# Last rows in 32-row transfers on two queues, two thirds of the angles together, and a new order of all steps

## The chip, the cores and the metric

The kernel runs on one core of a Trainium2 chip. A core has TensorE (PE in the profile), VectorE (DVE), ScalarE (ACT), GpSimd (POOL) and SyncE (SP), each with its own instruction stream, and 16 DMA engines that they share. The metric is the device time of one execution in microseconds (us), given as the median of three runs.

## The reference

Eight batches of 576 positions go through linear attention with 8 heads of 64, a norm over each head, and then a gated long convolution; all inputs and the output are float32.

```python
kv  = einsum('bhsd,bhse->bhde', k, v)          # 64x64 per head
out = einsum('bhsd,bhde->bhse', q, kv)
x   = out / sqrt(mean(out*out) + 1e-6) * g_norm  # then (batch, 576, 512)
x1, x2, x3 = split(x @ w_proj, 3)              # 512 columns each
conv = irfft(rfft(x2, 576) * rfft(filter, 576), 576)
y   = (x1 * conv * x3) @ w_out                 # (8, 576, 512)
```

## The kernel before

The work of a batch is cut into some ninety small steps, each a Python function that records a few instructions. The string `ORDER` names the steps one after another, as name.batch, with a third number where filler matmuls stand ahead of the step's own. The loop at the end of the kernel (line 798) calls them in that order, so `ORDER` alone sets the order of the instructions on every engine; the waits between engines follow from the tiles that they share. An engine runs its own instructions strictly in order. PSUM is held as four pairs of banks, and `take` (line 98) gives a step the pair that has been free longest; `free` gives it back when its contents have been copied out.

The steps that the prediction speaks of:

- **Loads.** `L...` steps issue the loads of q, k, v and the weights from GpSimd. `Zi` makes index rows there, `Zd` an identity matrix (`ident`), `Zr` turns it into `rev` on VectorE.
- **Tables.** `An0`, `An1`, `An2` call `angles` (line 227): per third of the frequencies three VectorE instructions and three ScalarE ones (Sin, Abs, Sin) fill `IV`, the table of sines and cosines. `Act` (line 244) loads ScalarE's second function table, which the norm's reciprocal square root needs. `Tb0` to `Tb2` transpose `IV` on TensorE and copy the result out, `Ff0` to `Ff2` fold the filter into `ff` (lines 309 to 324), `H0` to `H2` make the filter's spectrum from both.
- **A batch.** `K` forms kv, `O01` and `O23` the attention, `sq`, `R`, `rs`, `x` the norm, `Ga` and `Gb` the two gates x1 and x3 (line 640, a quarter of the channels each), `abM`, `rrM`, `F0`, `F1`, `F2` the forward transform of x2, `M0` to `M2` its product with the filter, `A0`, `A1` sums on GpSimd or, as `Av0`, `Av1`, on VectorE (line 621), `I` and `Io` the inverse transform, `f...` the last product into `yg`.
- **Output.** `U0`, `U2`, `U4` multiply `yg` by w_out, `ot` copies the result into one of five buffers, and SyncE sends it out in transfers of 32 rows (lines 732 and 745).
- **The last batch's end.** For batch 7 five tiles of 128 rows go another way: `V0` to `V3` (line 759) and `U4` multiply, `va`/`vv` (line 765) copy the tile to SBUF on ScalarE or VectorE, and `V_out` (line 772) sends it in two transfers, one of them of two or three times 32 rows: `[[2 * DM, n], [6 * DM, 32], [1, DM]]`. The step's name has the queue (s SyncE, g GpSimd, a ScalarE), then tile and piece: `dg31` is GpSimd's transfer of piece 1 of tile 3.

Tiles `kb`, `vb` and `sq`, which held k, v and squares before, serve as the output buffers of these five tiles.

Of the kernel before, what the change touches and what calls it, by code (L numbers as in the profile page):

```python
# [19 lines left out]
ORDER = """Z.0 Lqa.0 Zi.0 Lf.0 Zt.0 An2.0 An1.0 An0.0 Zd.0 Act.0 Zf.0 Zr.0 T0.0.18 Tb2.0 Lqb.0 Tb0.0 eTv0.0 Lva.0 Tb1.0.3 Ff0.0  # L20
Ff1.0 Ff2.0.2 Lka.0 Lvb.0 T1.0 Ka.0 Lkb.0 eKva.0 Lw3.0 eTa1.0 H1.0 O01.0 sq1.0 Lqa.1 Kb.0.7 sq0.0 Lw1.0 eKab.0 O23.0
ov0.0 sq3.0 ov1.0 R0.0.1 ov3.0 sq2.0 R1.0.2 rs0.0 ov2.0 R2.0 Lk.1 rs2.0 T0.1 R3.0.1 rs1.0 rs3.0 eTa0.1 Lv.1 x0.0 x1.0
eo1.0 H0.0 H2.0 Gb3.0 Ga3.0 HN1.0 Lqb.1 Ga1.0 eo0.0 K.1 x13.0 Lw2.0 g3.0 eK.1 Gb1.0 fr.0 Ga2.0 x11.0 T1.1 g1.0 HN0.0
x12.0 O01.1 rrM.0 rrT.0 eTa1.1 fa1.0 sq1.1 fa0.0 sq0.1 ob1.1 verr.0 abM.0 F0.0 abT.0 ov0.1 Lv.2 Lkb.2 eab.0 O23.1.2
eT.0 F2c.0 M0.0 F2.0 sq2.1 ob2.1 Lqa.3 Gb2.0 Lqb.3 Lka.2 F1t.0 Lq.2 M2.0 sq3.1 A0.0 F1.0 g2.0 R0.1 ob3.1 R2.1 Ga0.0
rs0.1 R1.1 rs2.1 x10.0 K.2 M1.0 R3.1 Gb0.0 Av1.0 rs1.1 rs3.1 x.1 eo.1 eK.2 I01.0 Io01.0 ea01.0 oa01.0 Io23.0.1 Qt.3
Qt.2 oa23.0 fr.1 I23.0 Qh.3 Ga0.1 ea23.0 g0.0 fa.1 vB.0 Ga1.1 w.0 f001.0 x11.1 rrM.1 x10.1 rrT.1 err.1 O01.2 Lk.3
f101.0 abT.1 sq0.2 ob0.2 f023.0 abM.1 sq1.2 Lvb.4 eT.1 Gb1.1 F0.1 ob1.2 g1.1 eab.1 O23.2 Lv.3 sq2.2 ob2.2 M0.1 Ga3.1
Lwo.0 sq3.2 Gb0.1 F2c.1 f123.0 ob3.2 F2.1 R3.2 x13.1 F1t.1 g0.1 R0.2 F1.1 rs3.2 M2.1 R2.2 rs0.2 rs2.2 R1.2 K.3 Gb3.1
rs1.2 Ga2.1 M1.1 g3.1 eK.3 O23.3 x12.1 sq2.3 sq3.3 Gb2.1 x.2 Lk.4 A0.1 Av1.1 Lva.4 ob3.3 U0.0 Io23.1 g2.1 I23.1 ob2.3  # L30
ot0.0 I01.1 eo0.2 Ga0.2 eo1.2 ea23.1 ea01.1 Lqb.5 fa0.2 ov23.1 Io01.1 R2.3 Lqa.5 oa01.1 fa1.2 xv0.2 abT.2 rs2.3 eT.2
O01.3 fr.2 abM.2 sq0.3 ob0.3 Ga3.2 rrM.2 vB.1 sq1.3 ob1.3 eab.2 R3.3 rrT.2 w.1 x13.2 f001.1 f101.1 f123.1 f023.1 rs3.3
Lqa.4 K.4 F1t.2 err.2 F1.2 eKm.4 R0.3 rs0.3 Gb0.2 M1.2 g0.2 F0.2 Gb3.2 Lqb.4 Ga1.2 U4.1 g3.2 x11.2 R1.3 rs1.3 A1.2
Ga2.2 F2c.2 Lk.5 Lv.5 M0.2 A0.2 Qt.4 Qt.5 ot4.1 x12.2 O23.4 F2.2 x.3 sq2.4 U2.0 ob2.4 Qh.5 M2.2 sq3.4 ot2.0 Gb2.2
I01.2 ov3.4 eo.3 Lqa.6 ea01.2 I23.2 Lqa.7 ea23.2 g2.2 Gb1.2 g1.2 fa0.3 Io23.2 Lqb.6 fa1.3 Io01.2 oa01.2 R3.4 oa23.2
U0.1 rs3.4 Lqb.7 abT.3 fr.3 O01.4 ot0.1 sq1.4 vB01.2 vB23.2 abM.3 sq0.4 veT.3 rrM.3 ob0.4 rrT.3 eab.3 F2c.3 w.2 K.5
ov1.4 err.3 F1t.3 F2.3 F1.3 R2.4 eK.5 rs2.4 fin.2 U2.1 M2.3 M1.3 Ga1.3 F0.3 R1.4 x1.4 ot2.1 x11.3 R0.4 Ga2.3 rs1.4
rs0.4 Gb1.3 x12.3 M0.3 O23.5 g1.3 Lv.6 Gb2.3 sq2.5 Ga3.3 Av0.3 x0.4 ob2.5 g2.3 U0.2 sq3.5 x13.3 Lk.6 A1.3 I23.3 eo0.4
eo1.4 I01.3 ob3.5 ot0.2 Ga0.3 ev23.3 fa0.4 fa1.4 ea01.3 Io01.3 x10.3 Io23.3 ov01.3 fr.4 oa23.3 Gb0.3 g0.3 abT.4 eT.4
K.6 O01.5 vB.3 Gb3.3 eK.6 sq1.5 ob1.5 sq0.5 abM.4 ob0.5 eab.4 w.3 rrM.4 rrT.4 F1t.4 Qt.7 F1.4 g3.3 R3.5 err.4 rs3.5  # L40
R2.5 Ga2.4 rs2.5 Qt.6 x12.4 R0.5 F0.4 fin.3 M1.4 R1.5 rs0.5 A1.4 M0.4 U2.2 rs1.5 Gb2.4 ot2.2 O23.6 F2c.4 x0.5 x1.5
Qh.7 U4.3 g2.4 sq2.6 Av0.4 F2.4 M2.4 eo0.5 Ga3.4 sq3.6 ob3.6 ob2.6 x13.4 Ga0.4 x10.4 ot4.3 U0.3 ot0.3 eo1.5 Io23.4
fr.5 I23.4 Gb3.4 oa23.4 I01.4 Io01.4 ev23.4 oa01.4 fa.5 g3.4 rrM.5 ea01.4 O01.6 sq0.6 rrT.5 vB.4 ob0.6 err.5 Lv.7
Gb0.4 g0.4 Ga1.4 abT.5 xv1.4 sq1.6 Gb1.4 R0.6 eT.5 w023.4 w001.4 ob1.6 rs0.6 Ga1.5 R3.6 g1.4 x11.5 w123.4 F0.5 abM.5
Lk.7 rs3.6 eab.5 w101.4 fin.4 R2.6 rs2.6 M0.5 Gb1.5 K.7 F1t.5 g1.5 F2c.5 eK.7 F1.5 Ga3.5 F2.5 A0.5 x13.5 U2.3 M1.5
M2.5 ot2.3 R1.6 Gb3.5 Ga2.5 g3.5 rs1.6 O23.7 A1.5 x.6 x12.5 U0.4 Gb2.5 sq3.7 ov3.7 sq2.7 ob2.7 ot0.4 R2.7 Io01.5 eo0.6
oa01.5 eo1.6 Ga0.5 g2.5 I23.5 fa.6 fr.6 rs2.7 x10.5 Io23.5 abT.6 ea23.5 I01.5 ov23.5 abM.6 ea01.5 Gb0.5 veT.6 vB.5
eab.6 O01.7 sq0.7 g0.5 sq1.7 F2c.6 ob1.7 F2.6 rrM.6 rrT.6 M2.6 err.6 F1t.6 w.5 F1.6 Ga0.6 ob0.7 R3.7 x10.6 Ga3.6 rs3.7
M1.6 x13.6 fin.5 F0.6 R1.7 rs1.7 R0.7 Gb3.6 rs0.7 Gb0.6 M0.6 g3.6 g0.6 U0.5 Av0.6 Ga1.6 x.7 U4a.5 A1.6 U4b.5 Io01.6
eo.7 ot0.5 x11.6 Ga2.6 oa01.6 ot4.5 fa0.7 x12.6 Io23.6 I01.6 ea01.6 I23.6 oa23.6 U2.5 Gb2.6 vB01.6 fa1.7 ea23.6 fr.7  # L50
g2.6 vB23.6 Gb1.6 g1.6 abM.7 ot2.5 w.6 rrM.7 eab.7 abT.7 fin.6 rrT.7 F2c.7 eT.7 F1t.7 err.7 F2.7 F1.7 U2.4 M1.7 ot2.4
Ga0.7 F0.7 M2.7 Ga1.7 x11.7 A1.7 Gb0.7 x10.7 U0.6 M0.7 Gb1.7 g0.7 Av0.7 I23.7 ot0.6 Io23.7 g1.7 Io01.7 Ga2.7 ov23.7
oa01.7 ev23.7 I01.7 vB23.7 w123.7 Gb3.7 Ga3.7 ea01.7 vB01.7 U2.6 w023.7 w101.7 w001.7 x13.7 g3.7 Gb2.7 x12.7 ot2.6
f101.7 V2a.7 g2.7 f123.7 V3.7 f001.7 V2b.7 va3.7 va2.7 V1a.7 f023.7 ds20.7 V1b.7 dg31.7 U4a.7 vv1.7 V0a.7 ds11.7
ds10.7 U4b.7 dg21.7 V0b.7 vv4.7 va0.7 ds30.7 dg00.7 ds40.7 ds41.7 ds01.7"""
# [3 lines left out]
def kernel(  # L59
# [167 lines left out]
    def angles(c):  # L227

        if 'ang' not in tmp:
            tmp['ang'] = work.tile([P, 2, 3, TH], FP32, name="ang", tag="tpw1")  # L230
# [2 lines left out]
        vec.tensor_scalar(out=a_, in0=tmp['tv'], scalar1=kturn[:, c:c + 1], scalar2=MAGIC, op0=ALU.mult, op1=ALU.add)
# [2 lines left out]
        act.activation(out=IV[:, 2 * c + 1], in_=a_, func=AF.Sin, scale=W0)
# [596 lines left out]
```

## Time and profile before

| | |
|---|---|
| median of 3 runs | 228.15 us (227.96 to 228.92) |
| the profiled execution | 227.85 us, of which the span from first to last instruction is 226.1 us |
| mean granted TensorE clock | 0.967 |
| TensorE busy | 202.1 us (89%) |
| VectorE busy | 183.6 us (81%) |
| ScalarE busy | 146.9 us (65%) |
| GpSimd busy | 59.2 us (26%) |
| read from and written to HBM | 33.69 MB and 9.44 MB |

The profile shows one execution. A group is named by its line of the kernel, engine, operation and tiles; a row of the timeline has start, duration, engine, line, operation and count, and in brackets the idle time ahead of it and what ended that. A row of the windows has a stretch of time, its length, the busy time and number of instructions of each engine, the granted TensorE clock, the mean busy share of the 16 DMA engines and the rate in GB/s. TensorE's matmuls overlap, so that a busy TensorE need not be TensorE at its peak. GpSimd's and SyncE's transfers are listed with the time of issuing them; the time "to landing" runs from the issue until the data is reported as written.

### The profile page before, as it was taken

Reading aid. Unit: us, or ns where it says so; the run is one execution under the profiler, and the core shown is the slowest. Engines: PE = TensorE matmul, PEld = TensorE weight load, DVE = VectorE, ACT = ScalarE, POOL = GpSimd, SP = SyncE. Lnnn points to the kernel's source line nnn. Section 1 sums busy time; section 2 is a strip of 40 time slices with the busy share of each in tenths; the row PEclk is TensorE's granted clock in tenths of the full one; section 3 lists DMA queues with packets and bytes.
Section 4 is the critical chain, followed back from the end, with each engine's and each line's share of the span. In section 5 each row is a group of like instructions: output and inputs, shape, how many; then the busy total and the mean of one; then the engine's idle time right before and its main releaser. Section 6 shows DMA issues by size and latency. Waiting matters only on the chain.

```text
span 226.1 us, 5000 instructions
## 1 busy us (share of the span) xinstructions
PE 202.1 (89%) x2042; PEld 119.9 (53%) x2042; DVE 183.6 (81%) x283; ACT 146.9 (65%) x235; POOL 59.2 (26%) x65
## 2 busy tenths in 40 slices
PE   7898999999999999999999999999999999995000
...
DMA  4999999999999499999458495005001433314410
GB/s 19 191 206 206 207 206 205 207 177 150 207 204 210 117 169 140 256 243 215 129 123 163 61 227 157 0 19 145 27 0 30 122 84 93 97 44 86 105 62 29
DMA packets 37414, 30.16 MB, mean 133 GB/s; under 512 B 16398, under 2 KB 32782, under 8 KB 37390
## 3 DMA queue, kind: packets, MB, share of 16 engines
...
q1 hardware_dynamic: 19694, 12.59, 23.4%
...
HBM read 33.69 MB, written 9.44 MB: 191 GB/s over the span
## 4 chain that ended last, share of the span: by engine, by line
PE 63%; issue 15%; DVE 5%; ACT 4%; POOL 3%; POOLq 0%; DVEq 0%; ACTq 0%
PE ps L640 21%; PE ps L725 7%; PE ps L552 6%; PE ps L670 4%; PE ps L463 3%; PE ps L456 3%; POOL Y L621 3%; PE ps L538 2%; PE ps L558 2%; PE ps L383 2%; DVE tpw L615 2%; PE ps L338 2%; PE ps L545 1%; PE ps L112 1%; PE ps L596 1%
## 5 line engine op out<-in xcount | busy, mean ns | idle before, releaser
L640 PE MATMUL ps<-x,wp 128*128 128x288 bf16 x512 | 70.8, 286 | 0.1
L640 PEld LDWEIGHTS <-wp 128*128 128x128 bf16 x512 | 48.9, 98 | 17.2 <-issue 1.9
L621 POOL TENSOR_TENSOR Y<-tpw 128x1024 bf16<-128x1024 f32 (+1 forms) x10 | 25.9, 2594 | 105.5 <-DVE tpw L615 105.5
L615 DVE TENSOR_TENSOR tpw<-ps,HH 97x2048 f32<-97x2048 f32 (+1 forms) x16 | 36.6, 2289 | 4.2 <-PE ps L596 2.3
L725 PE MATMUL ps<-wo,yg 128*128 128x512 bf16 x112 | 26.5, 379 | 0.0
L646 ACT CAST x<-ps 128x576 bf16<-128x576 f32 x30 | 19.0, 643 | 11.4 <-PE ps L640 9.7
L648 DVE TENSOR_TENSOR g<-ps,x 128x576 bf16<-128x576 f32 x32 | 23.9, 754 | 2.9 <-PE ps L640 1.8
L562 ACT CAST x<-ps 128x1024 bf16<-128x1024 f32 (+1 forms) x21 | 18.8, 895 | 10.3 <-PE ps L552 6.0
L729 ACT COPY ot<-ps 128x1024 f32<-128x1024 f32 x14 | 14.2, 1014 | 12.4 <-PE ps L725 12.3
L477 ACT ACTIVATE rstd<-ps 128x576 bf16<-128x576 f32 x32 | 20.1, 652 | 2.7 <-PE ps L463 2.4
L466 ACT ACTIVATE sq<-ps 128x576 bf16<-128x576 f32 x32 | 20.0, 653 | 2.2 <-PE ps L456 2.0
L674 ACT CAST ar<-ps 128x576 bf16<-128x576 f32 x25 | 15.1, 645 | 7.7 <-PE ps L671 6.8
L473 ACT ACTIVATE o<-ps,g_col 128x576 bf16<-128x576 f32 x24 | 17.7, 749 | 0.0
L725 PEld LDWEIGHTS <-yg 128*128 128x128 bf16 x112 | 10.8, 98 | 11.3 <-issue 0.5
L670 PE MATMUL ps<-IV,Y 128*128 128x192 bf16 x128 | 15.5, 245 | 0.0
L552 PE MATMUL ps<-wp,ab 128*128 128x512 bf16 x64 | 15.1, 380 | 0.0
L140 POOL DMA_DIRECT2D qb<-in_q_dram x15 | 10.5, 702 | 13.8 <-PE ps L425 12.0
L112 PE MATMUL ps<-nil,ind 128*128 128x512 bf16 x37 | 11.9, 458 | 1.6 <-DVE ind L194 1.6
L671 PE MATMUL ps<-IV,Y 97*128 97x96 bf16 x64 | 13.2, 207 | 0.0
L463 PE MATMUL ps<-sq,ind 128*128 128x288 bf16 x64 | 12.3, 286 | 0.4 <-DVE o L471 0.4
L510 DVE TENSOR_TENSOR eo<-x 128x576 bf16<-128x576 bf16 (+1 forms) x26 | 12.1, 522 | 0.1
L498 DVE TENSOR_TENSOR x<-o,rstd 128x1152 bf16<-128x1152 bf16 (+1 forms) x11 | 11.2, 1029 | 1.0 <-ACT rstd L477 1.0
...
## 6 DMA issues: line engine op xcount, KB each, us to landing
out_dram<-ot SPq DMA_DIRECT2D x56, 128.0 KB, 2.5
...
vb<-in_v_dram POOLq DMA_DIRECT2D x6, 576.0 KB, 12.2
...
kb<-in_k_dram POOLq DMA_DIRECT2D x4, 288.0 KB, 11.2
out_dram<-ot SPq DMA_DIRECT2D x12, 64.0 KB, 5.2
```

The source lines that it names most:

```text
L463: nc.tensor.matmul(r2[:, h, 0:TH], ind, sq()[:, j, h * TH:(h + 1) * TH], start=True, stop=True)
L466: act.activation(out=halves(sq()[:, j]), in_=tmp['o', b, j][:, :, 0:TH], func=AF.Square)
L477: act.activation(out=halves(rstd()[:, j]), in_=tmp['r', b, j][:, :, 0:TH], func=AF.Abs_reciprocal_sqrt, scale=1.0 / D, bias=1e-6)
L552: nc.tensor.matmul(pp[:, h], abt()[:, j, 2 * h * P:(2 * h + 1) * P], w2(j), start=(j == 0), stop=(j == NDC - 1))
L562: act.copy(out=o_(), in_=tmp[key, b])
L615: vec.tensor_mul(out=t_[:n], in0=xp[:n].unsqueeze(1).to_broadcast([n, 2, 2, DM]), in1=two)
L621: op(out=Yt()[:n, 2 * g:2 * g + 2], in0=t_[:n, ::-1, 0], in1=t_[:n, ::-1, 1])
L640: nc.tensor.matmul(pp[:, h, 0:TH], w_, x[:, j, h * TH:(h + 1) * TH], start=(j == 0), stop=(j == NDC - 1))
L646: ev0(out=x1, in_=pp[:, :, 0:TH])
L648: vec.tensor_mul(out=halves(g13t()[:, dc]), in0=pp[:, :, 0:TH], in1=x1)
L670: nc.tensor.matmul(pp[:, i, 0:SB], Y[:, 2 * g + h, cs], IV[:, 2 * g + h, 0:SB], start=(g == 1), stop=(g == 2))
L725: nc.tensor.matmul(pp[:, cc], ygt(b)[:, dc, b % 2 * 64 + c * P:b % 2 * 64 + (c + 1) * P], wo[:, dc], start=(dc == 0), stop=(dc == NDC - 1))
```

## The change

Three things are changed.

`V_out` now sends each of the five last tiles in four transfers of 32 rows, in the form that lines 732 and 745 already have, 20 in all; 9 go from SyncE and 11 from GpSimd. `angles` takes a range of thirds: two thirds are computed with the long VectorE instruction and all ScalarE instructions over both at once. And `ORDER` is a new string from its first word to its last: 725 steps in place of 714, among them 38 filler matmuls in place of 37.

```diff
-    def angles(c):
+    def angles(c0, c1):
...
-        a_, r_ = (tmp['ang'][:, i, c] for i in range(2))
-        h = c // 2
-        vec.tensor_scalar(out=a_, in0=tmp['tv'], scalar1=kturn[:, c:c + 1], scalar2=MAGIC, op0=ALU.mult, op1=ALU.add)
-        vec.tensor_scalar(out=r_, in0=a_, scalar1=MAGIC, scalar2=-2.0 * S, op0=ALU.subtract, op1=ALU.mult)
-        vec.scalar_tensor_tensor(out=a_, in0=tmp['tv'], scalar=kcol[:, c:c + 1], in1=r_, op0=ALU.mult, op1=ALU.add)
-        act.activation(out=IV[:, 2 * c + 1], in_=a_, func=AF.Sin, scale=W0)
-        act.activation(out=r_, in_=a_, func=AF.Abs)
-        act.activation(out=IV[:, 2 * c], in_=r_, func=AF.Sin, scale=cosb[:, 2 + h:3 + h], bias=cosb[:, h:h + 1])
+        a_, r_ = tmp['ang'][:, 0], tmp['ang'][:, 1]
+        cs = slice(c0, c1)
+        for c in range(c0, c1):
+            vec.tensor_scalar(out=a_[:, c], in0=tmp['tv'], scalar1=kturn[:, c:c + 1], scalar2=MAGIC, op0=ALU.mult, op1=ALU.add)
+        vec.tensor_scalar(out=r_[:, cs], in0=a_[:, cs], scalar1=MAGIC, scalar2=-2.0 * S, op0=ALU.subtract, op1=ALU.mult)
+        for c in range(c0, c1):
+            vec.scalar_tensor_tensor(out=a_[:, c], in0=tmp['tv'], scalar=kcol[:, c:c + 1], in1=r_[:, c], op0=ALU.mult, op1=ALU.add)
+        act.activation(out=IV[:, 2 * c0 + 1:2 * c1:2], in_=a_[:, cs], func=AF.Sin, scale=W0)
+        act.activation(out=r_[:, cs], in_=a_[:, cs], func=AF.Abs)
+        for h, x, y in ((0, c0, min(c1, 2)), (1, 2, c1)):
+            if x < y:
+                act.activation(out=IV[:, 2 * x:2 * y - 1:2], in_=r_[:, x:y], func=AF.Sin, scale=cosb[:, 2 + h:3 + h], bias=cosb[:, h:h + 1])
...
     def V_out(b, key, i, q):
-        if key == 4:
-            bb, blk, i0, n = b - 1 + i, (NB - 2, 0)[i], 2 * i, 2
-        else:
-            x0 = 2 * (b % 2) + 4 * key
-            cut = 3 - x0 % 3 if x0 % 3 else 3
-            i0, n = ((0, cut), (cut, 4 - cut))[i]
-            bb, blk = b, x0 + i0
-        rows = bass.AP(tensor=out.tensor, offset=out.offset + (bb * S + t_of(blk)) * DM, ap=[[2 * DM, n], [6 * DM, 32], [1, DM]])
-        q.dma_start(out=rows, in_=tmp['ot', b, key][32 * i0:32 * (i0 + n)])
+        rows = o_rows(b - 1 + i // 2, (NB - 2, NB - 1, 0, 1)[i]) if key == 4 else o_rows(b, 2 * (b % 2) + 4 * key + i)
+        q.dma_start(out=rows, in_=tmp['ot', b, key][32 * i:32 * i + 32])
...
-        for i in range(2):
+        for i in range(4):
             for e, q_ in (("s", nc.sync), ("g", nc.gpsimd), ("a", nc.scalar)):
```

The first words of the two strings, up to the first attention step:

```diff
-Z.0 Lqa.0 Zi.0 Lf.0 Zt.0 An2.0 An1.0 An0.0 Zd.0 Act.0 Zf.0 Zr.0 T0.0.18 Tb2.0 Lqb.0 Tb0.0 eTv0.0 Lva.0 Tb1.0.3 Ff0.0
-Ff1.0 Ff2.0.2 Lka.0 Lvb.0 T1.0 Ka.0 Lkb.0 eKva.0 Lw3.0 eTa1.0 H1.0 O01.0
+Z.0 Zi.0 Zd.0 Zr.0 Lqa.0 Zt.0 An2.0 An01.0 T0.0.21 Lf.0 eTv0.0 Zf.0 Tb0.0.4 Tb1.0 Tb2.0 Lqb.0 Lva.0 Ff0.0 Ff2.0.2
+Ff1.0 Act.0 T1.0 Lka.0 Ka.0 eKa.0 eTv1.0 H1.0 Lkb.0 O01.0
```

The first place is ScalarE at the start of the program, from the last third of the angles on (IV is the table of sines, yg here holds the folded filter, FW, FY, FZ the transposed tables). Before:

```order
L236 ACTIVATE IV<-ang 128x288
L237 ACTIVATE ang<-ang 128x288
L238 ACTIVATE IV<-ang,cosb 128x288
L245 ACT_TABLE_LOAD
L287 COPY FY<-ps_67 128x128
L288 COPY FZ<-ps_67 128x64
L289 COPY FW<-ps_67 32x768
L289 COPY FW<-ps_68 128x768
L323 CAST yg<-ps_67 128x1024
L323 CAST yg<-ps_68 128x1024
```

Now:

```order
L239 ACTIVATE IV<-ang 128x2x288
L240 ACTIVATE ang<-ang 128x576
L243 ACTIVATE IV<-ang,cosb 128x2x288
L294 COPY FW<-ps_67 128x768
L292 COPY FY<-ps_69 128x128
L293 COPY FZ<-ps_69 128x64
L294 COPY FW<-ps_69 32x768
L328 CAST yg<-ps_66 128x1024
L328 CAST yg<-ps_68 128x1024
L250 ACT_TABLE_LOAD
```

The table load has moved from between the sines and the copies to behind the last of the copies, and the last three sine instructions work on two thirds.

The second place is GpSimd's start. Before, its first work was a load of q:

```order
L140 DMA qb_74<-in_q_dram 96x4x384
L204 ISA
L204 IOTA ki 128x1
L207 IOTA tvi 128x192
L208 IOTA tvi 128x96
L307 DMA fn<-in_moe_filter_fft_dram 96x3072
masks.py:197 MEMSET ident 128x128
masks.py:199 AFFINE_SELECT ident<-ident 128x128
```

Now:

```order
L205 ISA
L205 IOTA ki 128x1
L208 IOTA tvi 128x192
L209 IOTA tvi 128x96
masks.py:197 MEMSET ident 128x128
masks.py:199 AFFINE_SELECT ident<-ident 128x128
L141 DMA qb_74<-in_q_dram 96x4x384
L312 DMA fn<-in_moe_filter_fft_dram 96x3072
```

The load of q stands behind the index rows and the identity.

The third place is the end of the two queues that send rows out. GpSimd before:

```order
L621 TENSOR_TENSOR Y<-tpw 97x1024
L621 TENSOR_TENSOR Y<-tpw 128x1024 x3
L781 DMA out_dram<-vb_73 3x32x512
L781 DMA out_dram<-vb_72 2x32x512
L781 DMA out_dram<-kb_70 32x512
```

and now, where the sums of batch 7 end with one of the 97-row kind, which VectorE did before:

```order
L626 TENSOR_TENSOR Y<-tpw 128x1024 x3
L626 TENSOR_TENSOR Y<-tpw 97x1024
L779 DMA out_dram<-vb_73 32x512 x2
L779 DMA out_dram<-vb_72 32x512
L779 DMA out_dram<-kb_70 32x512 x3
L779 DMA out_dram<-vb_72 32x512
L779 DMA out_dram<-vb_73 32x512
L779 DMA out_dram<-kb_71 32x512
L779 DMA out_dram<-vb_72 32x512
L779 DMA out_dram<-kb_71 32x512
```

SyncE before:

```order
L781 DMA out_dram<-vb_72 2x32x512
L781 DMA out_dram<-kb_71 32x512
L781 DMA out_dram<-kb_71 3x32x512
L781 DMA out_dram<-vb_73 32x512
L781 DMA out_dram<-sq 2x32x512 x2
L781 DMA out_dram<-kb_70 3x32x512
```

and now:

```order
L779 DMA out_dram<-vb_73 32x512
L779 DMA out_dram<-vb_72 32x512
L779 DMA out_dram<-kb_70 32x512
L779 DMA out_dram<-sq 32x512 x3
L779 DMA out_dram<-kb_71 32x512 x2
L779 DMA out_dram<-sq 32x512
```

The ten transfers, three of them GpSimd's, have become twenty, eleven of them GpSimd's. Each queue cycles through eight completion counters, so that its ninth transfer waits until its first has landed: GpSimd's ninth to eleventh wait for its first to third.

77 lines of the change are left out of this document (39 added, 38 removed).

## The prediction

> **What bounds the kernel now.** I read the engines' shares first, then the slices, the windows, the end of the timeline with the transfers issued there, and last the start.
>
> ```profile
> PE 202.1 (89%) x2042; PEld 119.9 (53%) x2042; DVE 183.6 (81%) x283; ACT 146.9 (65%) x235; POOL 59.2 (26%) x65
> PE   7898999999999999999999999999999999995000
> DMA  4999999999999499999458495005001433314410
> ```
>
> TensorE is the bound from the first tenth until it stops in slice 37 of 40; the last three slices hold no matmul and few transfers. The windows show how dense the middle is:
>
> ```profile
> 30.00:60.00 30.00, 29.88 (x369) 18.10 (x368) 27.33 (x34) 24.78 (x43) 8.56 (x10) 1.00 1.20 190
> 90.00:120.00 30.00, 29.95 (x360) 18.04 (x357) 29.14 (x44) 23.10 (x38) 6.43 (x7) 1.00 0.95 195
> 150.00:180.00 30.00, 30.00 (x236) 19.47 (x234) 28.30 (x38) 21.27 (x32) 5.63 (x2) 1.00 0.23 63
> ```
>
> TensorE's idle time there is 0.12, 0.05 and 0.00 us of 30. So a new order has almost nothing to win between 30 and 180 us; it can only lose. What can be won lies in front of and behind that. The end, from the timeline, the windows and SyncE's waits:
>
> ```profile
> 205.84 0.59 PE L763 MATMUL ps<-wo,yg 128*128 128x512 bf16 x2
> 206.47 0.58 ACT L769 COPY kb<-ps 128x512 f32<-128x512 f32 x1 [1.95 <-PE ps L763]
> ...
> 208.31 3.62 SPq L781 DMA_DIRECT2D out_dram<-sq  x2
> 212.04 2.02 SPq L781 DMA_DIRECT2D out_dram<-kb  x1
> ```
> ```profile
> 206.00:208.00 2.00, 0.43 (x3) 0.00 (x0) 0.69 (x1) 0.58 (x1) 0.53 (x1) 1.00 0.58 67
> 214.00:216.00 2.00, 0.00 (x0) 0.00 (x0) 0.00 (x0) 0.00 (x0) 0.00 (x0) 0.50 0.18 62
> 220.00:222.00 2.00, 0.00 (x0) 0.00 (x0) 0.00 (x0) 0.00 (x0) 0.00 (x0) 0.50 0.13 51
> ```
> ```profile
> SPq L828 <- DMA out_dram<-sq: 8.1, 1, 8.1
> SPq L828 <- DMA out_dram<-kb: 2.5, 1, 2.5
> ```
>
> The last matmul ends at 205.84 + 0.59 = 206.43, the last copy at 207.05, and the span at 226.06 (the page rounds to 226.1): 19.6 us behind the last matmul in which only rows go out. SyncE issues until 214.06 and then waits 8.1 + 2.5 us, to 224.66, so 1.4 us follow the last landing. Meanwhile the transfers move 51 to 67 GB/s with 0.13 to 0.18 of the DMA engines busy, two to three of 16. That is no limit of bandwidth: those engines are serving long strings of rows, 32 for each leading index of the two- and threefold pieces, and the others are idle. The transfers issued there, and the 32-row ones of earlier batches (line 745, duration of issue and then landing):
>
> ```profile
> out_dram<-vb POOLq DMA_DIRECT2D x1, 192.0 KB, 8.0
> out_dram<-vb POOLq DMA_DIRECT2D x1, 128.0 KB, 9.0
> out_dram<-kb SPq DMA_DIRECT2D x1, 64.0 KB, 9.1
> out_dram<-kb POOLq DMA_DIRECT2D x1, 64.0 KB, 7.1
> out_dram<-vb SPq DMA_DIRECT2D x1, 64.0 KB, 9.7
> ```
> ```profile
> L745 SPq DMA_DIRECT2D out_dram<-ot x12: 325/421/573, 85.5 to 177.3; - x12
> DMA to landing us min/median/max: 1.7/5.2/6.7
> ```
>
> The same SyncE transfer of 32 rows lands in 1.7 us at best, in 5.2 as a median beside loads, and in 9.1 and 9.7 behind the long strings.
>
> **Part 1, the start.** Before, the chain runs through the last set of sines, the table load and the first copy:
>
> ```profile
> 8.12 0.44 ACT L236 ACTIVATE IV<-ang 128x288 bf16<-128x288 f32 x1
> 9.57 1.28 ACT L245 ACT_TABLE_LOAD   x1
> 10.87 0.27 ACT L287 COPY FY<-ps 128x128 bf16<-128x128 bf16 x1
> ```
> ```profile
> 1.32 0.85 POOL L140 DMA_DIRECT2D qb<-in_q_dram  x1 [0.87 <-POOLq L817]
> 2.26 0.15 POOL L204 IOTA ki<- 128x1 int32 x1
> 3.61 0.32 POOL masks.py:199 TENSOR_SCALAR_AFFINE_SELECT ident<-ident 128x128 bf16<-128x128 bf16 x1
> 3.81 0.37 DVE L233 TENSOR_SCALAR ang<-tv,kturn 128x288 f32<-128x288 f32 x1
> 15.97 1.21 DVE L323 CAST yg<-ps 32x1024 bf16<-32x1024 f32 x1 [0.75 <-PE ps L321]
> 18.70 1.11 ACT L349 ACTIVATE hu<-ps,cf 128x1024 f32<-128x1024 f32 x1 [1.00 <-PE ps L338]
> ```
>
> In the change GpSimd makes index rows and identity first, from 1.32 on; they took 2.26 to 3.93 with the filter's load of 0.5 between, so the first load of q comes some 1.2 us later. VectorE makes `rev` before the indices and so starts the angles about 0.5 us later than 3.81; its long instruction over two thirds gives back about half of that. So it ends near 8.15. ScalarE then needs a set of three instructions, 8.12 to 9.57 = 1.45 us for one third. Over two thirds each has 288 more elements; a copy of 512 takes 0.58 (line 769), a pass over 1024 takes 1.11 (line 349), so 288 are 0.3 and three times that 0.9. The sines end near 10.4, 0.8 later than before. But the 1.28 us of table load no longer stand before the copies. They stand behind both copies of the folded filter, ahead of kv's copies: hidden as far as VectorE and TensorE still work on the rest of the filter, which came at 15.97 + 1.21 = 17.18 before. By my count the folded filter is complete near 16 us, the table load ends near 17.3, and the first product with it (line 349) starts near 17.9 in place of 18.70. I take 0.8 us of gain; bounds are a loss of 1.0 (cover of the table load gone, and the later q shows) and a gain of 1.8 (0.5 of table load, the rest as well).
>
> **Part 2, the middle.** A row of fillers, and the gap where TensorE goes between full and 64-row matmuls:
>
> ```profile
> 18.96 1.69 PE L112 MATMUL ps<-nil,ind 128*128 128x512 bf16 x7
> ```
> ```profile
> PEld L456 <- issue: 4.3, 14, 0.4
> ```
>
> Seven fillers hold TensorE 1.69 us, of which the last one's own passage is about 0.2: 0.22 each. Behind the first R there are 5 in place of 7: a gain of 0.4. The gaps are 4.3 us over 14, 0.3 each. By the new order there are 35 stretches of such matmuls in place of 33: a loss of 0.6. VectorE gives three copies of `ar` to ScalarE and two sums to GpSimd, gets two copies of qT and one of `ot`: a little lighter, and off the path while TensorE has no gaps. The two sums are the new risk; bound and price from this group:
>
> ```profile
> L621 POOL TENSOR_TENSOR Y<-tpw 97x1024 bf16<-97x1024 f32 x4 | 10.3, 2574 | 28.1 <-DVE tpw L615 28.1
> ```
>
> A sum on GpSimd takes 2.6 us and TensorE's inverse transform waits for all of Y. If it is late, the wait is at most 2.6 for each sum; if other matmuls cover it, 0. I allow 0.5 for this and every other new gap together.
>
> **Part 3, the last tiles on TensorE.**
>
> ```profile
> 201.50 0.76 DVE L648 TENSOR_TENSOR g<-ps,x 128x576 bf16<-128x576 f32 x1 [0.38 <-ACT ot L729]
> 202.81 1.90 PE L763 MATMUL ps<-wo,yg 128*128 128x512 bf16 x8 [0.55 <-DVE yg L692]
> ```
>
> Before, two matmuls stood ahead of the product that the last gate (0.76) gives, TensorE idled 0.55, and 18 matmuls followed (202.81 to 205.84 are 14 of them, 0.216 each). Now four stand ahead and 16 follow: two matmuls, 0.43, go into the idle time, of which I count 0.35. So the last matmul ends at 206.43 - 0.8 - 0.4 + 0.6 + 0.5 - 0.35 = 206.0, between 204.5 (start at its best, no new gap) and 210 (start at its worst, one sum late).
>
> **Part 4, the drain.** Tile 3 is ready 12 matmuls before the end, 2.6 us; with its copy (0.58) GpSimd's first issue is at 204.1. Eleven issues follow one another. Rows for their spacing:
>
> ```profile
> 204.34 1.42 POOL L781 DMA_DIRECT2D out_dram<-vb  x2 [13.44 <-ACT vb L769]
> 207.35 0.53 POOL L781 DMA_DIRECT2D out_dram<-kb  x1 [1.59 <-ACT kb L769]
> ```
>
> 0.71 for the large ones, 0.53 for 32 rows. I take 0.62: the eleventh starts at 204.1 + 6.2 = 210.3. How long a 32-row transfer from GpSimd takes to land when no string is in its way, no row shows. Below it lies SyncE's 1.7, above it GpSimd's 7.1, which was behind two strings. SyncE's went from 9.1 and 9.7 to 1.7 without them, so I lean to the low end and take 2.5. Then the last lands at 212.8, and with 1.4 the span ends at 214.2. SyncE's last three issues start behind the last copy (206.6) 0.42 apart and land by 209.2; they do not decide. Eight counters do not bite either: GpSimd's ninth, tenth and eleventh wait for its first three, which have landed by 208.
>
> The Trainium skill ("DMA: Bandwidth & Descriptors", section "Why a DMA increments its semaphore by 16 and not by 1") says that a transfer runs on the largest number of engines up to 16 that divides the slowest dimension of both sides: 2 and 3 for the old pieces, 16 for 32 rows, on either queue; the windows' two to three busy engines agree. Its section on the anatomy of a GpSimd transfer fits 2.0 us plus bytes over 436 GB/s, an estimate of 2.15 for 64 KB; the sum by that would be 0.35 us shorter. No run here shows it yet.
>
> The span goes from 226.06 to 214.2. The profiled execution took 227.85, 1.79 more than its span, which gives 216.0; the median of the runs lies 0.3 above that execution, so **216.3 us** is the forecast.
>
> **The rivals.**
>
> A: GpSimd's transfers still land in 7.1 us, because what makes them slow is GpSimd's way of writing descriptors and not the strings. For it: all three of its transfers took 7 to 9, the smallest too. Against it: the smallest was issued third, behind the two large ones. Then the counters bite: the third issue, at 205.3, lands at 212.4; the eleventh starts there and lands at 219.5; the span ends at 220.9, the time is 222.7, with the 0.3 **223.0**.
>
> B: the new order leaves gaps on TensorE. Place: the sums of the last batches, now one after the other on GpSimd ahead of the inverse transform. Two sums late cost 5.2: **221.5**. For it: GpSimd's row above; against it: gates and output matmuls stand between.
>
> C, the slower side: small transfers on one queue do not overlap, so that GpSimd's eleven cost their landing one after another. The span would be 204.1 + 11 x landing + 1.4; it decides from (226.06 - 205.5) / 11 = 1.87 us per transfer, and with 2.5 the time is **235.1**. For it: SyncE's issues of 3.62 for two and 2.02 for one at the end, a queue that is backed up. Against it: those had strings before them, and line 745's issues took 0.42 with landings of 5.2.
>
> The Trainium skill ("DMA: Bandwidth & Descriptors", section "Bandwidth") speaks for C: batch to a mebibyte, a transfer of 64 KB costs 0.95 us. Twenty of these in a row are an estimate of 19 us, about what the drain takes now, and the change would be worth 1 us or less. The rows of line 745 speak against reading it as a cost in series.
>
> **How the numbers follow.** The forecast (drain of 7 to 10 us behind the last matmul, that one at 204.5 to 208) has 0.60, A 0.17, B 0.14, C 0.05, and 0.04 is left for an order that costs more than 10 us somewhere in the middle. Low end: last matmul at 204.5, spacing 0.53, landing 1.7: 204.5 - 1.9 + 5.3 + 1.7 + 1.4 + 2.1 = 213.1. High end: rival A, 223.0, which takes in B. Under 0.5% (1.1 us) nothing can be told from no change. A and B are both faster than 227.0, so faster has 0.60 + 0.17 + 0.14 + a share of the rest = 0.93, no change 0.02, slower 0.05.
>
> **What would show it.** In the changed profile the last stretch should show 0.4 or more of the DMA engines busy and over 150 GB/s until about 212, landings of 2 to 3 us for 32 rows on both queues, and GpSimd's issues 0.5 to 0.7 apart without a wait for its own transfers. A gap in GpSimd's row before the ninth means A; issues of SyncE over 1 us each mean C. At the start the second table load should stand near 16 us and the first product of the spectrum before 18.5. In the windows from 30 to 180 TensorE's idle time should stay under 0.5 us in all. The prediction is wrong if the drain stays above 12 us or the last matmul ends after 208.

## The result and the profile after

The changed kernel takes **217.41 us** (median of 4 runs, 217.00 to 218.32), the kernel before 228.06 us beside it (227.62 to 228.92). The ratio is 0.9534, 95% interval 0.9491 to 0.9577. The forecast was 216.3, from 213.1 to 223.0.

The time and its sign agree with the prediction, but the sum behind it does not hold term by term, and the last matmul ends at 209.38, past the 208 beyond which the prediction called itself wrong. The profiled execution took 218.32 us with a span of 216.6. First its shares and slices of the span, as on the page before:

```profile
PE 204.0 (94%) x2043; PEld 120.4 (56%) x2043; DVE 183.6 (85%) x278; ACT 146.4 (68%) x235; POOL 68.2 (32%) x75
PE   7999999999999999998999996999999999999960
...
DMA  4999999999999495999999719300330120426074
```

TensorE now works until slice 39 of 40, and the DMA engines are busy behind it. Two slices of its row that were full before now read 8 and 6 (from zero, 18 and 24): gaps that were not there. The end of the timeline (start, duration, engine, line, work), and the windows around it (TensorE, weight loads, VectorE, ScalarE, GpSimd busy, granted clock, busy share of the DMA engines, GB/s):

```profile
207.71 1.54 POOL L779 DMA_DIRECT2D out_dram<-vb  x3 [10.49 <-ACT vb L774]
208.35 1.03 PE L768 MATMUL ps<-wo,yg 128*128 128x512 bf16 x4
...
212.65 0.50 POOL L779 DMA_DIRECT2D out_dram<-kb  x1
```
```profile
206.00:208.00 2.00, 2.00 (x11) 0.87 (x10) 0.80 (x3) 1.07 (x2) 0.29 (x1) 1.00 0.82 227
208.00:210.00 2.00, 1.38 (x7) 0.41 (x5) 0.38 (x1) 1.17 (x2) 2.00 (x5) 1.00 0.75 195
210.00:212.00 2.00, 0.00 (x0) 0.00 (x0) 0.00 (x0) 0.00 (x0) 2.00 (x5) 1.00 0.75 203
212.00:214.00 2.00, 0.00 (x0) 0.00 (x0) 0.00 (x0) 0.00 (x0) 1.15 (x3) 0.60 0.76 242
```

The last matmul ends at 208.35 + 1.03 = 209.38, and 216.6 - 209.38 = 7.2 us follow in place of 19.6. The drain gave 12.4 us, and TensorE took 2.95 of it back: its last matmul ended at 206.43 before and was to end at 206.0. The transfers of the last stretch, size and median landing:

```profile
out_dram<-vb POOLq DMA_DIRECT2D x6, 64.0 KB, 2.3
out_dram<-kb POOLq DMA_DIRECT2D x5, 64.0 KB, 2.6
out_dram<-sq SPq DMA_DIRECT2D x4, 64.0 KB, 2.2
```

GpSimd's transfer of 64 KB lands in 2.3 to 2.6 us where it took 7.1 behind the long strings. Its eleven issues stand (212.65 - 207.71) / 10 = 0.494 apart and none waits for a transfer.

**Where TensorE lost time.** Two of the windows, then the rows around the gaps: TensorE's first row behind each, and what VectorE and GpSimd did meanwhile.

```profile
90.00:120.00 30.00, 29.12 (x357) 17.91 (x356) 27.12 (x38) 22.25 (x38) 6.55 (x4) 1.00 1.13 217
120.00:150.00 30.00, 28.30 (x277) 16.97 (x274) 27.58 (x30) 20.14 (x31) 8.62 (x6) 1.00 0.38 82
```
```profile
99.69 0.78 PE L388 MATMUL ps<-vb,kb 64*64 64x64 bf16 x72 [0.85 <-DMA kb<-in_k_dram]
...
129.38 2.34 POOL L626 TENSOR_TENSOR Y<-tpw 97x1024 bf16<-97x1024 f32 x1
129.41 3.60 DVE L515 TENSOR_TENSOR eo<-x 128x1152 bf16<-128x1152 bf16 x2
132.93 1.21 DVE L635 TENSOR_TENSOR Y<-ps,HM 128x1024 bf16<-128x1024 f32 x1
134.19 1.14 PE L645 MATMUL ps<-x,wp 128*128 128x288 bf16 x8 [1.67 <-DVE Y L635]
```

The gap of 0.85 waits for k of batch 5. Its load stands in GpSimd's row behind a sum and three other loads:

```profile
82.03 2.35 POOL L626 TENSOR_TENSOR Y<-tpw 128x1024 bf16<-128x1024 f32 x1 [17.16 <-DVE tpw L620]
84.34 0.72 POOL L141 DMA_DIRECT2D qb<-in_q_dram  x1
85.06 0.77 POOL L145 DMA_DIRECT2D vb<-in_v_dram  x1
85.81 0.68 POOL L141 DMA_DIRECT2D qb<-in_q_dram  x1
86.47 1.51 POOL L145 DMA_DIRECT2D kb<-in_k_dram  x2
```

In the old order it was issued at 84.21, directly behind the sum. It landed at 90.47 there and at 99.64 here.

The gap of 1.67 waits for a pair of PSUM banks that VectorE's third product (line 635) frees. The product is late because the two sums of halves ahead of it (line 515) took 3.60 in place of twice 0.75. That line by itself:

```profile
L515 DVE TENSOR_TENSOR eo<-x x20: 445/750/2925, 26.0 to 178.9; 128x1152 bf16<-128x1152 bf16 x12, 128x576 bf16<-128x576 bf16 x8
```

One of its instructions took 2.925. It began 0.03 after GpSimd's sum of batch 4, and ran on for 0.6 when that sum had ended at 131.72. The new order moved this sum (A0 of batch 4) from VectorE to GpSimd. With two gaps of 0.30 and 0.17 near 41 these make 2.99 us; in all, TensorE idles 3.19 us from 30 to 180, where it idled 0.17 before.

### The profile page after: what moved, and what is told of

Its sections match the earlier page's. It is cut to its first block, busy times and chain, and to the rows that moved or that the text cites. A ratio compares the mean times of both kernels' runs of the same rounds, so it can differ in the third digit from the quotient of the medians.

```text
span 216.6 us, 5016 instructions
## 1 busy us (share of the span) xinstructions
PE 204.0 (94%) x2043; PEld 120.4 (56%) x2043; DVE 183.6 (85%) x278; ACT 146.4 (68%) x235; POOL 68.2 (32%) x75
## 4 chain that ended last, share of the span: by engine, by line
PE 65%; issue 9%; DVE 7%; DMA 6%; POOL 6%; ACT 5%; POOLq 0%; ACTq 0%
PE ps L645 21%; PE ps L730 7%; DMA kb<-in_k_dram 6%; PE ps L113 5%; PE ps L557 4%; PE ps L675 3%; DVE tpw L620 3%; PE ps L543 3%; PE ps L468 2%; POOL out_dram L779 2%; PE ps L388 2%; POOL Y L626 2%; DVE eo L515 2%; PE ps L343 2%; PE ps L563 2%
## 5 line engine op out<-in xcount | busy, mean ns | idle before, releaser
L626 POOL TENSOR_TENSOR Y<-tpw 97x1024 bf16<-97x1024 f32 (+1 forms) x12 | 31.0, 2586 | 89.6 <-DVE tpw L620 89.6
L679 ACT CAST ar<-ps 128x576 bf16<-128x576 f32 x28 | 17.1, 643 | 9.7 <-PE ps L676 9.6
L471 ACT ACTIVATE sq<-ps 128x576 bf16<-128x576 f32 x32 | 20.1, 655 | 2.7 <-PE ps L461 2.6
L734 ACT COPY ot<-ps 128x1024 f32<-128x1024 f32 x13 | 13.2, 1015 | 8.2 <-PE ps L730 8.1
L141 POOL DMA_DIRECT2D qb<-in_q_dram x13 | 9.6, 746 | 17.0 <-PE ps L468 10.8
L515 DVE TENSOR_TENSOR eo<-x 128x1152 bf16<-128x1152 bf16 (+1 forms) x20 | 14.5, 770 | 0.1
L697 DVE TENSOR_TENSOR yg<-w,g 128x576 bf16<-128x576 bf16 (+1 forms) x20 | 12.0, 632 | 0.1
```

Source lines behind the costliest of these rows:

```text
L471: act.activation(out=halves(sq()[:, j]), in_=tmp['o', b, j][:, :, 0:TH], func=AF.Square)
L626: op(out=Yt()[:n, 2 * g:2 * g + 2], in0=t_[:n, ::-1, 0], in1=t_[:n, ::-1, 1])
```

## The experiments

Two theories stand against each other. The first: the drain and the body are separate. The shape of the pieces alone made the drain long, and the new order costs about 3 us through one late load and one sum at a bad moment. The second: the change is one thing. The new order is part of what shortens the drain, and its gaps are only the places at which a nearly full VectorE shows. The first eight runs are told apart by the part they touch; the last two put parts together.

### The drain in the old order

```diff
 (the kernel before, with its own order)
-    (ten transfers of two- and threefold pieces)
+    rows = o_rows(b - 1 + i // 2, (NB - 2, NB - 1, 0, 1)[i]) if key == 4 else o_rows(b, 2 * (b % 2) + 4 * key + i)
+    q.dma_start(out=rows, in_=tmp['ot', b, key][32 * i:32 * i + 32])
-... va2.7 V1a.7 f023.7 ds20.7 V1b.7 dg31.7 ... ds41.7 ds01.7
+... va2.7 ds30.7 dg31.7 V1a.7 f023.7 ds32.7 dg33.7 V1b.7 ds20.7 dg21.7 ... ds02.7 dg03.7
```

> The kernel before, with its own order of all steps and its own start; only the last rows go out in twenty transfers of 32 rows, ten by SyncE and ten by GpSimd. Theory (drain and body are separate, the long strings alone made the drain long): the last matmul ends at 206.4 as before, GpSimd issues about 0.5 apart from 204.3 on, the last rows are issued near 209 and land 2.3 to 2.6 later, the span ends near 213 and the time is about 214.9, 2.5 less than the change. Rival (the short drain needs the new order of the last tiles): more than 10 us behind the last matmul, time 218 or more.

Measured: **214.03 us**, ratio 0.9388 (0.9367 to 0.9409), span 212.4. It is faster than the whole change. The end of its timeline and two windows:

```profile
204.37 2.03 POOL L774 DMA_DIRECT2D out_dram<-vb  x4 [13.43 <-ACT vb L769]
205.88 0.59 PE L763 MATMUL ps<-wo,yg 128*128 128x512 bf16 x2
...
207.86 0.99 POOL L774 DMA_DIRECT2D out_dram<-kb  x2
```
```profile
206.00:208.00 2.00, 0.48 (x3) 0.00 (x0) 0.69 (x1) 0.59 (x1) 2.00 (x5) 1.00 0.92 264
208.00:210.00 2.00, 0.00 (x0) 0.00 (x0) 0.00 (x0) 0.00 (x0) 0.84 (x2) 1.00 0.86 260
```

The last matmul ends at 206.47, as before, and 5.9 us follow. So the new order of the last tiles is not needed for the short drain. With ten issues on each queue, GpSimd is done at 208.85 instead of 213.15, and the transfers move 260 GB/s with 0.9 of the DMA engines busy.

### The old pieces in the new order

```diff
 (the changed kernel, with V_out of the kernel before)
-... va2.7 ds30.7 f023.7 V0b.7 vv0.7 dg31.7 U4.7 ds22.7 ds02.7 dg33.7 ... (20 transfers)
+... va2.7 ds30.7 f023.7 V0b.7 vv0.7 dg31.7 U4.7 ds20.7 dg00.7 ds01.7 V1.7 dg21.7 va4.7 ds40.7 va1.7 ds41.7 ds11.7 ds10.7
```

> The changed kernel with its order and its start, but its last rows go out in the ten two- and threefold pieces of the kernel before, five by SyncE and five by GpSimd less one (as before: seven and three). Theory: the last matmul ends at 209.4 as in the changed kernel, 19.6 us follow as before, the time is about 230.8, 1.2% slower than before. Rival (the new order itself shortens the drain): 15 us or less behind the last matmul, time 226 or less.

(The ten pieces go out as seven by SyncE and three by GpSimd.) Measured: **230.52 us**, ratio 1.0102 (1.0066 to 1.0138): slower than before. The last matmul and the landings:

```profile
207.59 1.03 PE L767 MATMUL ps<-wo,yg 128*128 128x512 bf16 x4
```
```profile
out_dram<-vb POOLq DMA_DIRECT2D x1, 192.0 KB, 7.5
...
out_dram<-kb POOLq DMA_DIRECT2D x1, 64.0 KB, 7.4
```

The last matmul ends at 208.62 and 20.1 us follow (span 228.7). The new order with its new start costs 2.6 us here (230.52 against 227.94 for the kernel before beside it). The drain's gain comes from the pieces alone.

### The same transfers with a leading index of two

```diff
-        rows = o_rows(...)
...
+        rows = bass.AP(tensor=out.tensor, offset=out.offset + (bb * S + t0 + 96 * (i % 2)) * DM, ap=[[(t1 - t0) * DM, 2], [6 * DM, 16], [1, DM]])
         q.dma_start(out=rows, in_=tmp['ot', b, key][32 * i:32 * i + 32])
```

> The changed kernel with the same twenty transfers of 32 rows, 64 KB each, on the same queues, but each one's destination is two groups of 16 rows in two neighbouring blocks, so that its leading index runs over 2. (Every row of the output is written, but within a pair of blocks rows change places; nothing is left out.) Theory (the leading index of 2 or 3 leaves the transfer to 2 or 3 of the DMA engines, size and number do not matter): landings rise to 5 us or more, the windows behind the last matmul show two to four busy engines and under 100 GB/s, the drain is 14 us or more in place of 7.2, the time 224 to 231. Rival (the old pieces were slow because they were large, 128 and 192 KB): landings of 2.3 to 2.6 and 217.4 as in the changed kernel.

Measured: 227.61 us (one run), span 225.8, 18 us behind the last matmul at 207.99. Size, number and queues are those of the change; the destination's leading index is 2 and not 32, and rows change places within a pair of blocks.

```profile
out_dram<-vb POOLq DMA_DIRECT2D x6, 64.0 KB, 5.7
out_dram<-kb POOLq DMA_DIRECT2D x5, 64.0 KB, 6.2
```
```profile
212.00:216.00 4.00, 0.00 (x0) 0.00 (x0) 0.00 (x0) 0.00 (x0) 1.51 (x3) 0.59 0.57 131
216.00:220.00 4.00, 0.00 (x0) 0.00 (x0) 0.00 (x0) 0.00 (x0) 0.00 (x0) 0.50 0.17 60
220.00:224.00 4.00, 0.00 (x0) 0.00 (x0) 0.00 (x0) 0.00 (x0) 0.00 (x0) 0.50 0.12 41
```
```profile
211.74 0.60 POOL L782 DMA_DIRECT2D out_dram<-kb  x1 [0.63 <-DMA out_dram<-vb]
```

0.17 and 0.12 of 16 engines are 2.7 and 1.9 engines. They are not that few throughout: from 210 to 216 the share is 0.57 to 0.58. That is the picture of the kernel before, with 0.60 from 210 to 212 and 0.13 to 0.20 from 214 to 222. So neither the size nor the number of transfers is the cause. The profile of the kernel before has a control that the prediction passed over: line 732 also sends two blocks of 32 rows, 128 KB, but with 32 as the leading index and the 2 behind it.

```profile
out_dram<-ot SPq DMA_DIRECT2D x56, 128.0 KB, 2.5
```

These land in 2.5 us, where GpSimd's piece of 128 KB with a leading 2 took 9.0. The queue and the moment differ, but twice the size and a second block do not make a transfer slow. The last row of the run also shows rival A's mechanism at work: GpSimd's ninth issue waits 0.63 for one of its own transfers once these land slowly. In the change they land in time and it does not wait.

The Trainium skill ("DMA: Bandwidth & Descriptors", section "Why a DMA increments its semaphore by 16 and not by 1") gives the largest number up to 16 that divides the slowest dimension of both sides as the number of engines: 2 here, 16 for 32 rows. The traces fit: 1.9 to 2.7 engines' worth at the end of this run, 0.75 to 0.92 of the 16 with a leading 32. Its section "Bandwidth", which spoke for rival C, gives 0.95 us for 64 KB, measured on loads; an estimate from that for the twenty in series was 19 us. In the change the twenty went out in 7.5, from the first issue (207.44) to the last landing (214.90), so it does not hold as a cost in series.

### The load of k first

```diff
-... Qt.4 Lqa.7 g2.2 ... veT.3 Lk.5 f123.2 ...
+... Qt.4 Lk.5 g2.2 ... veT.3 Lqa.7 f123.2 ...
```

> The changed kernel with the load of k of batch 5 in the place of half a load of q of batch 7, directly behind a sum on GpSimd, and that half load in the other's place. Theory (TensorE's 0.85 us idle at 98.83 is this load's late issue): issued near 84.4 in place of 86.5 the load lands by 97.6, the gap is gone, the one at 132.5 stays; the last matmul ends near 208.5, the time is about 216.6. Rival 1 (the transfer is held by other loads, not by its place): the gap stays at 0.5 or more. Rival 2 (VectorE sets the pace, and a gap closed opens elsewhere): the gap is gone and the last matmul still ends at 209.4.

Measured: 216.79 us, ratio 0.9508 (0.9484 to 0.9531).

```profile
83.47 0.80 POOL L145 DMA_DIRECT2D kb<-in_k_dram  x1
```
```profile
90.00:120.00 30.00, 29.93 (x360) 17.71 (x358) 27.74 (x39) 22.91 (x39) 6.73 (x5) 1.00 1.14 220
120.00:150.00 30.00, 28.33 (x276) 17.34 (x273) 27.43 (x31) 19.80 (x31) 9.94 (x5) 1.00 0.32 71
```

TensorE's idle time from 90 to 120 falls from 0.88 to 0.07 and stays at 1.67 from 120 to 150. The load lands at 90.14 in place of 99.64: the gap was the load's place in the row, not the transfer. The size of the gap varies: the six profiles with the load in its late place have 0.22 to 0.86, the two with k first (this one and the mended kernel) none. In the median time alone, this run can't be told from the change (0.9508 and 0.9534, with intervals that overlap). The last matmul ends at 207.62, 0.9 earlier than expected; that part comes from the start (below).

### The sum of batch 4 on VectorE, and beside another instruction

First the sum back on VectorE:

```diff
-... eo.5 M2.4 ob3.6 U0.3 A0.4 Ga1.4 ...
+... eo.5 M2.4 ob3.6 U0.3 Av0.4 Ga1.4 ...
```

> The changed kernel with one sum, the first of batch 4, on VectorE in place of GpSimd (where the kernel before had it). Theory (VectorE's sum of halves waited out GpSimd's sum, 2.92 in place of 0.75, and TensorE idled 1.66 for the bank behind it): the two sums of halves take 0.75 each, VectorE's bank is free near 132.1, the gap at 132.53 is gone; VectorE then works 1.2 more, and the last matmul ends near 207.7, time about 215.8. Rival (VectorE is the limit there by its amount of work): with 1.2 more on VectorE a gap of 1 to 2 us stays in that stage, and the last matmul ends at 209 or later.

Measured: 215.60 us, ratio 0.9452 (0.9426 to 0.9478), last matmul 207.02.

```profile
129.02 1.43 DVE L515 TENSOR_TENSOR eo<-x 128x1152 bf16<-128x1152 bf16 x2
130.36 1.22 DVE L635 TENSOR_TENSOR Y<-ps,HM 128x1024 bf16<-128x1024 f32 x1
131.50 1.22 DVE L626 TENSOR_TENSOR Y<-tpw 97x1024 bf16<-97x1024 f32 x1
```

Second, the sum left on GpSimd and VectorE's next two changed about:

```diff
-... sq3.6 eo.5 M2.4 ob3.6 U0.3 A0.4 ...
+... sq3.6 M2.4 eo.5 ob3.6 U0.3 A0.4 ...
```

> The changed kernel with two neighbours on VectorE changed about: the third product of batch 4 (one operand in PSUM, it frees the bank TensorE waits for at 132.53) ahead of the sums of halves of batch 5 (both operands in SBUF). GpSimd's sum stays where it is and runs beside them. Theory (a VectorE instruction with two operands in SBUF waits out a sum on GpSimd; one with an operand in PSUM does not): the product takes its 1.21 beside the sum, the bank is free near 130.7, TensorE's gap of 1.66 is gone, and the first sum of halves still waits for the end of GpSimd's sum (1 us or more over its 0.75); last matmul near 207.7, time about 215.7. Rival (a sum on GpSimd slows whatever VectorE does): the product takes 2 us or more and a gap of 0.5 or more stays.

Measured: 215.39 us, ratio 0.9431 (0.9407 to 0.9454), last matmul 206.52.

```profile
128.34 2.34 POOL L626 TENSOR_TENSOR Y<-tpw 97x1024 bf16<-97x1024 f32 x1
```
```profile
129.63 1.23 DVE L635 TENSOR_TENSOR Y<-ps,HM 128x1024 bf16<-128x1024 f32 x1 [1.29 <-ACT ot L747]
130.77 1.42 DVE L515 TENSOR_TENSOR eo<-x 128x1152 bf16<-128x1152 bf16 x2
```

In both the sums of halves take 1.42 or 1.43 for two, not 3.60, and the large gap is gone. Giving VectorE 1.2 us more work made the kernel faster by 1.8 (the gap was 1.67 of it), so it was not VectorE's amount of work. The stall itself comes again in every profile that keeps this order, with 2.93 or 2.94 for the same instruction in four more. In the second, the product (one operand in PSUM) takes its 1.23 although GpSimd's sum runs beside it until 130.68: a sum does not slow every instruction. The other half of that expectation was missed at this place. The product waited 1.29 for a bank, so the sums of halves began when GpSimd's sum was over. But the same profile has the wait again later: a sum of halves of 576 columns that starts near 153.9 takes 1.06 in place of 0.45, beside a sum on GpSimd that ends at 154.62. The clash also runs the other way, and it was there before the change. In the profile before, the sums on GpSimd at 85.74 and 168.13 took 3.09 and 3.41 in place of 2.35; each began while VectorE worked on an instruction with both operands in SBUF (85.25 to 86.60, 167.96 to 169.31).

The Trainium skill ("SBUF — State Buffer", section "SBUF: two separate sides") says that VectorE and GpSimd share one pair of ports as a lock: of an instruction of VectorE with two operands in SBUF and a GpSimd instruction that reads SBUF, the one that starts first holds it to its end, and the other waits. The traces agree, both ways: 2.9 us for an instruction of 0.75, which could go on when the sum had ended at 131.72, 3.1 to 3.4 for a sum that came second, and no wait for the product with one operand in SBUF.

### The start

Two executions of the new start stand apart by 0.86 us. The fillers, the first transposes of the sine tables and the first gate, first in the change's profile and then in that of the run with k first:

```profile
1.62 7.65 PE L113 MATMUL ps<-nil,ind 128*128 128x512 bf16 x21 [1.62 <-DVE ind L195]
9.11 0.68 PE L430 MATMUL ps<-ident,qb 96*128 96x96 bf16 x12
...
10.48 0.50 PE L281 MATMUL ps<-ident,IV 128*128 128x128 bf16 x6
...
28.79 2.38 PE L645 MATMUL ps<-x,wp 128*128 128x288 bf16 x18
```
```profile
1.61 6.33 PE L113 MATMUL ps<-nil,ind 128*128 128x512 bf16 x21 [1.61 <-DVE ind L195]
7.78 0.68 PE L430 MATMUL ps<-ident,qb 96*128 96x96 bf16 x12
...
9.61 0.51 PE L281 MATMUL ps<-ident,IV 128*128 128x128 bf16 x6 [0.28 <-ACT IV L243]
...
27.93 3.24 PE L645 MATMUL ps<-x,wp 128*128 128x288 bf16 x25
```

In both, the fillers begin at 1.61 to 1.62 and stand 0.43 apart; later they stand 0.22 apart. The step comes at 7.56 in the first and at 4.98 in the second. The twenty-one fillers then give way to the transposes of q at 9.11 or at 7.78. Four more fillers stand behind these, and the sine tables, ready at 9.56, wait until 10.48 or don't. Seven executions of the new start, with the step's time and the first gate's:

```
spacing halves at   4.57   4.98   4.98   6.29   6.55   7.52   7.56
first gate at      27.95  27.93  27.95  28.14  28.18  28.71  28.79
```

The Trainium skill ("TensorE: Matmul & The Clock Gate", section "Part 1: The HAM clock gate") says that TensorE starts at half rate and is let up after a busy window of about 3.4 us that runs freely, so that the same kernel steps up at varying times. The traces agree in the half rate and in the varying moment, but the earliest step comes 2.95 us after the first filler (4.57 - 1.62), sooner than such a window. The profile's granted clock reads 1.00 in these windows and does not show it.

A run with fewer fillers:

```diff
-T0.0.21
+T0.0.14
```

> The changed kernel with 14 fillers in place of 21 ahead of the first transposes on TensorE. In the profile of the change the fillers start 0.43 apart and go to 0.22 apart at 7.56, so that they end at 8.9 and hold the transposes; in that of the run with k of batch 5 first the same fillers go to 0.22 at 4.98 and end at 7.6, and everything behind stands 0.86 earlier. Theory (seven fillers less end by 8 even at the slow spacing): the first transposes of the sine tables start at 9.6, the first product of the spectrum near 18.1, the first gate near 27.9, whenever the spacing changes; time 0.4 to 0.9 under the change's 217.4. Rival (with less work TensorE speeds up later and the transposes run slow): first gate at 28.8 or later, no gain.

Measured: 217.91 us, ratio 0.9538 (0.9497 to 0.9580): no gain. In the profiled execution the start came as expected (step at 6.21, first gate at 27.93, 216.96 us), and of the four two took 216.7 and 217.0, but the other two took 218.9, with a mean granted clock of 0.982 and 0.983 where the first two have 0.990 and 0.989. What cost these 2 us no profile shows; it stays open.

And the start's change alone in the old order:

```diff
 (the kernel before, with angles() of the change)
-Z.0 Lqa.0 Zi.0 Lf.0 Zt.0 An2.0 An1.0 An0.0 Zd.0 Act.0 ... Ff1.0 Ff2.0.2
+Z.0 Lqa.0 Zi.0 Lf.0 Zt.0 An2.0 An01.0 Zd.0 ... Ff1.0 Act.0 Ff2.0.2
```

> The kernel before with the start's change alone: angles of two thirds in one set of instructions, and the table load behind the folded filter in place of ahead of it; all other steps in the old order, the old pieces at the end. Theory of the prediction (0.8 us): the first gate starts near 28.0 in place of 28.81, the last matmul ends near 205.6, the time is about 227.1. Rival (the table load is only moved, from ahead of the filter's copies to ahead of the copies of k times v, and TensorE waits for these instead): first gate at 28.6 or later, time 227.9 as before.

Measured: 227.71 us, ratio 0.9987 (0.9965 to 1.0010), not to be told from before. In its profile the table load stands at 15.19 and the first gate at 28.44, 0.37 earlier than before: between the two expectations.

### The parts put together

The changed kernel with its places mended (k first, the product ahead of the sums of halves, ten transfers on each queue as the tiles come):

```diff
-... Qt.4 Lqa.7 ... veT.3 Lk.5 ... sq3.6 eo.5 M2.4 ...
+... Qt.4 Lk.5 ... veT.3 Lqa.7 ... sq3.6 M2.4 eo.5 ...
-... va2.7 ds30.7 f023.7 V0b.7 vv0.7 dg31.7 ...
+... va2.7 ds30.7 dg31.7 f023.7 V0b.7 vv0.7 ds32.7 dg33.7 ...
```

> The changed kernel with three places mended together: k of batch 5 loaded in the place of half of q of batch 7, the third product of batch 4 ahead of the sums of halves of batch 5, and the last twenty transfers given out as in the old order with 32 rows (ten each, alternating as the tiles come). Theory (gaps and drain add up): both gaps of TensorE gone, the last matmul ends between 205.8 (start as in the run with k first) and 206.7 (start as in the change's profile), 5.9 us follow, time 213.5 to 214.4, 3.4 under the change. Rival (VectorE, 85% busy, sets the middle's pace and opens another gap): last matmul at 207.5 or later, time 215.2 or more.

Measured: **214.25 us**, ratio 0.9393 (0.9371 to 0.9415).

```profile
90.00:120.00 30.00, 29.92 (x358) 17.80 (x356) 27.75 (x39) 23.06 (x38) 6.73 (x5) 1.00 1.14 219
120.00:150.00 30.00, 30.00 (x289) 18.37 (x287) 27.08 (x31) 20.46 (x33) 9.95 (x5) 1.00 0.34 74
```

Both gaps are gone, no other has opened (the two near 41, 0.47 together, are still there), the last matmul ends at 206.04, and 6.3 us follow. GpSimd's sum and VectorE's load of work are as in the change. The second theory falls.

Last, the old order with both other parts:

```diff
 (the kernel before)
+ angles of two thirds together, Act.0 behind Ff1.0
+ the last rows in twenty transfers of 32, as in the first run
```

> The kernel before, in its old order, with the two other parts of the change: the angles of two thirds together with the table load behind the folded filter, and the last rows in twenty transfers of 32. Theory (parts add up): 214.03 less the 0.37 that the first gate came earlier in the profile of the start alone, 213.7. Rival (the start is worth nothing in the median, as the times of the start alone say): 214.0.

Measured: **213.71 us**, ratio 0.9371 (0.9351 to 0.9391), last matmul 206.06, first gate 28.42. It has the lowest median of this study and beats both kernels. Its interval overlaps those of the first run and of the mended order, so the 0.3 us of the start is not shown beyond its profile.

## Why the prediction was right, and where its sum was not

The forecast of the time held, and the long strings as the cause of the drain, which is most of the gain, were right. The sum was not, and the prediction's own signs say so. It called itself wrong if the last matmul ended after 208: it ended at 209.38. It put the second table load near 16 and the first product of the spectrum before 18.5: they stood at 17.08 and 18.93. It allowed 0.5 us of idle time from 30 to 180: there were 3.19. The signs for the drain came true within a few tenths. That the median lies only 1.1 us above the forecast is in part luck: the drain was shorter than counted and made up for some of this.

**Part 1, the start, 0.8 us: right as a mechanism, absent in the profiled execution.** In five other executions of the same start the first product of the spectrum came at 18.07 to 18.32, some 0.2 to 0.4 behind the count of 17.9, and in a sixth, with a late step, at 18.86. What the count left out is the row of 21 fillers ahead of the first transposes, three more than before, and the four behind them. Its sines were off the other way: they ended at 9.56, as before, and not near 10.4. VectorE had the angles at 7.37 in place of the 8.15 of the count: GpSimd's index rows began at 0.84 and not at 1.32, and the long instruction saved more than counted. In the old order the start's change alone moved the first gate by 0.37 and 0.38 (28.44 and 28.42 against 28.81 and 28.80), about half of the 0.8. The prediction gives a filler 0.22, from a later place of the trace; at the start it is 0.43 until a moment that varies. The old start has slack there and is deaf to it: with the step at 6.57 its transposes of the tables began at 9.61, when these were ready.

**Part 2, the middle, 0.5 us for all new gaps: wrong, 3.0.** This is the step that failed. I argued that a sum moved to GpSimd can at most be late for the inverse transform, 2.6 each, and that gates cover it. That never happened. The cost came by another way: one sum stopped a VectorE instruction that began 0.03 us later, and VectorE then held a bank that TensorE needed (1.67). The second cause, a load put behind three others (0.85), I had not looked for, though this part was the place to do so: half loads of q of batches 7 and 6 and a load of v had been set ahead of k of batch 5. The runs took each of the two gaps away by itself; those near 41 were left as they were. The 2.6 us for a sum is a mean over sums of 2.35 to 2.50 and one of 3.09, the one that waited for VectorE, so the clash stood in the row that the part was read from. The other two terms of this part (fillers, stretches of 64-row matmuls) were not measured apart. The row for the 64-row stretches counts waits of the weight loads (PEld); TensorE itself idled 0.17 us from 30 to 180 in that profile, so the row does not show the 0.3 us for each stretch.

**Part 3, the last tiles, 0.35: confirmed.** From the end of the last gate's matmuls to the end of the last matmul the traces show 4.6 us (204.77 to 209.38) in place of 5.0 (201.39 to 206.43).

**Part 4, the drain: right, and better by 1.0.** Predicted 8.2 us behind the last matmul, measured 7.2. Landings of 2.3 to 2.6 against 2.5; the spacing of GpSimd's issues 0.494 against 0.62, which over ten steps is 1.3. The bound of 0.53 was already above it. The prediction read the drain before as two to three busy engines throughout. That holds from 214 us on; its own row from 206 to 208, which has the 67 GB/s, shows 0.58 of the engines busy, and from 208 to 212 they were busy to 0.44 and 0.60.

So the last matmul came 3.4 later than forecast (209.38 against 206.0), the drain was 1.0 shorter, and the span of the profiled execution was 216.6 against 214.2. That execution was the longest of the four; the median is 1.1 above the forecast. The errors of the middle and of the drain have opposite signs, and the third, the start, varies from execution to execution.

**The rivals.** A (landings stay at 7.1) did not come; the run with a leading index of two shows what it would have looked like. B (gaps from the new order, by sums on GpSimd) came beside the short drain, right in its kind and at a third of its size (1.67 of 5.2), wrong in its place: not the last batches but batch 4, and not late but in the way. C (no overlap of small transfers) did not come: 0.75 of the DMA engines were busy.
